# State products with swapped operands in a fused attention and state-space kernel, and another choice of VectorE's share of the exponentials

## The chip, the core and the metric

The kernel runs on one core of a Trainium2 chip. The core has five engines that run side by side, each through its own queue and in order: TensorE (PE, matrix products into PSUM), VectorE (DVE), ScalarE (ACT), GpSimd (POOL) and SyncE (SP, which here issues the DMAs). The metric is the device time of one execution in microseconds; lower is better. Runs of one kernel are summed up by their median.

## The reference

A gate `g` mixes the output of an attention `a` with that of a state-space convolution `b`; both read the same `x` (2048 rows, 512 columns, bfloat16).

```python
g = sigmoid((x * gate_w).sum(-1, keepdims=True))
# a: 32 heads of 16 columns, softmax over 2048 keys
qkv = (x @ wqkv)...; scores = q @ k.T * 16 ** -0.5
a = (softmax(scores) @ v) @ wo
# b: a convolution of every column with a kernel of length 2048
P = exp((dt * A)[:, :, None] * l)          # A complex, 512 x 128 states
K = einsum("dn,dnl,dn->dl", C, P, dt * B).real
b = irfft(rfft(x padded) * rfft(K padded))[:2048] + x * Dskip
out = g * a + (1 - g) * b
```

## The kernel before

**Attention.** The 32 heads run in 32 blocks: a block is 4 heads against 512 queries. A block has 16 key tiles of 128 keys, called quads, since each has 4 tiles of scores (one a head, 128 keys by 512 queries). That makes 2048 tiles. They are worked off in 683 groups of three. In a group TensorE writes three score tiles into one of two PSUM buffers (`SC0`, `SC1`; `qk`), and ScalarE takes the exponentials of all three in one instruction (`ex`, L893) into `ET`. TensorE then multiplies `ET` by the values `VE` and adds up in the PSUM buffer `OA` (`pv`, `pv_mm`). Block 0 to 31 follow one another, 21.3 groups each. At a block's end VectorE transposes and normalises (`norm_a`, `norm_b`, `norm_c`).

**VectorE's sets.** Some quads are not done by ScalarE. VectorE computes the exponentials' bit patterns: one `tensor_scalar` for each of the four tiles from PSUM to a buffer `DZ` (`bits`, L927), and two more passes over all four (`batch`, L938) that give two shifted patterns. The three patterns are multiplied by `VE` and by two scaled copies of it (`VS`, made in `vscaled`) and added. Four groups in a row give one of their three tiles to VectorE, and ScalarE's instruction has two tiles there. Which quads may be taken is set by `VKT` (positions in a block), `WIN` (ranges of group numbers with the number of `DZ`/`DU` buffer pairs in each), `LEFT` (so many quads must be left in the block) and `DVQ`: the planner keeps count of VectorE's idle time in its own cost model, and a set is begun when the unspent idle time reaches a price. The price depends on which flag has been set: first .7, after `S15` (all state products done) 1.2, after `scan0` 2.0, after `scan1` .4 (`decide`, `clear`, `quad`).

**The state-space part** runs beside it, in the gaps. The sequence is cut into 32 chunks of 64 positions; the 512 columns are cut into 16 blocks of 32. First VectorE computes powers of the state factors (`params`, `base`, `table`): a table `PT` a block, written to memory (`ptd`, L1203) and read back transposed as `Qt` (`qload`). `kstage` makes the convolution's kernel within a chunk (`K0` to `K15`). `sstage` makes the state that each chunk adds: products of `Qt` with chunks of `x` (`X2`) into the PSUM buffer `MB`, four times a block ("banks"); VectorE multiplies by the signs `sgn` and writes `Sst` (L1264), a DMA writes that to `sd` in memory (L1270), and when a block is complete `sload` reads it back by a DMA transpose (L1290) into `SG0` or `SG1`, eight blocks each, which hold for every chunk two rows of `SGH` elements. `scan` then runs over the chunks on VectorE, first over `SG0` (`scan0`), then over `SG1` (`scan1`), and replaces each chunk's addition by its state. `ystage` multiplies the states by `Py` (read from `ptd`) and adds the products within a chunk (`Tt`, `XY`), in 32 units; VectorE evicts (L1399). At the end the two halves are mixed (L1525, L1538, L1719).

**Order.** A Python program writes all five queues ahead of time. Each stage is a generator ("thread") with a priority; it yields segments with an engine and an estimated cost, and conditions (`AFTER` a flag, `LOCK` on `MB`). After each group, `Sched.fill` issues the segments that fit before ScalarE's next instruction by estimated times. TensorE gets products of zeros (`zero`) up to a wanted amount of work a group (`FILL`); in groups below 425 whose number modulo 14 is below 4 (`REST`), no segment of priority 2 or 5 goes to TensorE, and the wanted amount is 1792. `place` lays the buffers into SBUF by the first and last group that uses them.

Of the kernel before, what the change touches and what calls it, by code (L numbers as in the profile page):

```python
# [13 lines left out]
P = 128  # L14
# [14 lines left out]
REST = (14, 4, 1792, 425)  # L29
# [7 lines left out]
SGH = 272  # L37
# [3 lines left out]
VKT = (1, 5, 9, 13)  # L41
SHAPE = ((2, 1),) * 4
LEFT = 4
VSW = 152
VSP = len(VKT) * VSW
# [363 lines left out]
def declare(nc, es):  # L409
# [11 lines left out]
    sb("VS", 2 * 4 * VSP)  # L421
    sb("ET", NS * 512)
    for w, (_, _, n) in enumerate(WIN):
        for r in range(n):
            sb(f"DZ{w}{r}", 2048)
            sb(f"DU{w}{r}", 2048)
# [61 lines left out]
    sb("Sst", 4 * 512)  # L488
# [19 lines left out]
    for n, free in (("ptd", NBLK * P * 2 * CB * T), ("sd", D * NCH * 2 * P),  # L508
                    ("kpd", NBLK * P * 8 * P), ("xrd", S * D), ("ytd", D * S), ("qd", D * S), ("od", D * S)):
        B[n] = Buf(n, "dr", free, BF16)  # L510
        B[n].t = nc.dram_tensor("gm_" + n, [free // P, P], BF16)
# [95 lines left out]
def record(nc, p, B, ins):  # L607
    KT, Qm, VE, VS, ET, OT, ON, Rz = (B[n] for n in ("KT", "Qm", "VE", "VS", "ET", "OT", "ON", "Rz"))
    OnT = [B[f"OnT{k}"] for k in range(4)]
    OA, MB = B["OA"], B["MB"]  # L610
    SC = [B["SC0"], B["SC1"]]
# [126 lines left out]
    todo, pend, rem, ends = [], [], [], {}  # L738
    plan = dict(b=-1, at=0, used=0.0, prev=None, wait=None, set=None, k=0)
# [7 lines left out]
    def win(x):  # L747
        return next((w for w, (lo, hi, _) in enumerate(WIN) if lo <= x < hi), None)

    def clear(x):  # L750
        w = win(x)
        if w is None or len(rem) < LEFT + 1 or not any(q % 16 in VKT for q in rem):
            return False
        mine = [i for i, st in enumerate(sets) if st["w"] == w]
        return len(mine) < WIN[w][2] or f"dvp{mine[-WIN[w][2]]}" in sch.flag

    def quad():
        if not rem:
            plan["b"] += 1
            plan["wait"] = None  # L760
            rem.extend(16 * plan["b"] + k for k in sorted(range(16), key=lambda k: (k in VKT, k)))
# [4 lines left out]
        if rem or q < NQ - 16:  # L766
            todo.append((q, plan["prev"], plan["wait"]))
# [15 lines left out]
    def decide(g):  # L783
        while len(tiles) < min(3 * g + 3, NSL):
            x = len(tiles) // 3
            plan["used"] = max(plan["used"], idle() - DVCAP)
            if plan["set"] is None and clear(x) and idle() - plan["used"] >= dvq():
                plan["used"] += dvq()
                c = next(q for q in rem if q % 16 in VKT)
                rem.remove(c)  # L790
# [3 lines left out]
                plan["set"], plan["k"], plan["wait"] = len(sets), 0, f"dvp{len(sets)}"  # L794
# [101 lines left out]
    def pv_mm(s, t, off, R, c, step=None):  # L896
# [6 lines left out]
        else:  # L903
            v, at, rv = VS, (4 * step + pi) * VSP + VKT.index(kt) * VSW, [(VS, (step, pi))]
# [3 lines left out]
    def vscaled():  # L908
        yield ("AFTER", f"g{WIN[0][0] - 12}")
        for pi in range(4):  # L910
            for step, (_, f) in enumerate(STEP):
                yield ("DVE", .3)
                op("DVE", lambda v, pi=pi, step=step, f=f: v.tensor_scalar(VS((4 * step + pi) * VSP, [[VSW, len(VKT)], [1, VSW]]),
                                                                           VE(pi * 4 * VG + VKT[0] * VW, [[VG, len(VKT)], [1, VSW]]), f, None, ALU.mult),
                   [(VE, (pi, x)) for x in range(16)], [(VS, (step, pi))], c=.3)
        sch.mark("VS")
# [16 lines left out]
    def batch(i):  # L933
# [17 lines left out]
        yield ("AFTER", "VS")  # L951
# [293 lines left out]
    Sst, sd = B["Sst"], B["sd"]  # L1245

    def sstage(blk):
        yield ("AFTER", f"ub{blk // 4}")
        q0, qr, bl = (blk % 2) * PTN, blk // 4, blk % 4
        for bank in range(4):  # L1250
            if blk:
                yield ("AFTER", f"sd{blk - 1}.{bank}")
            yield ("LOCK", "MB")
            for pp in range(2):
                yield ("PE", .2)
                for j in range(4):
                    k, par = 4 * bank + 2 * pp + j // 2, j % 2
                    mm(lambda pp=pp, j=j: MB(256 * pp, [[1, 256]], 32 * j, 32),
                       lambda k=k, par=par: X2[qr](16 * bl + k, [[64, 32]], 64 * par, 64),
                       lambda k=k, par=par: Qt(q0 + 128 * k, [[16 * 128, 2], [1, 128]], 64 * par, 64),  # L1260
                       [(Qt, (blk % 2, k // 8), blk), (Qt, (blk % 2, 2 + k // 8), blk), (X2[qr], par)], [(MB, 0, ('S', blk, bank))], pos=(64 * par, 32 * j),
                       c=.19 if j == 0 else 0, a=32, cfg="H")
            yield ("DVE", .65, -1)
            op("DVE", lambda v, bank=bank: v.tensor_tensor(Sst(512 * bank, [[256, 2], [1, 256]]), MB(0, [[256, 2], [1, 256]]),  # L1264
                                                           B["sgn"](0, [[0, 2], [1, 256]]), ALU.mult),
               [(MB, 0, ('S', blk, bank)), (B["sgn"], 0)], [(Sst, bank, (blk, bank))], c=.605)
            sch.unlock("MB")

            def put(bank=bank):
                dma("SP", lambda e, bank=bank: e.dma_start(sd.dram((CB * blk + 8 * bank) * 8192, [[256, P], [4 * 8192, 2], [1, 256]]),  # L1270
                                                           Sst(512 * bank, [[256, 2], [1, 256]])),
                    [(Sst, bank, (blk, bank))], [(sd, (blk, bank))], c=1., lat=3.)
# [484 lines left out]
```

## Time and profile before

| | us |
|---|---|
| median of 3 runs | 861.26 |
| lowest, highest | 856.72, 862.4 |
| the profiled execution, whole | 858.9 |
| its span in the profile | 857.1 |
| ScalarE busy | 832.4 |
| VectorE busy | 764.3 |
| TensorE busy (matmul) | 731.9 |

The profile is that of one execution. A row of a group of instructions gives line, engine, operation, output and inputs with shapes, the count after an x, then busy time and mean duration in ns, then the idle time just before them and what ended it. Instructions of one engine overlap at their ends, so the pace, start to start, is shorter than a duration. Rows of the chain of waits in order of time give start, length, engine, tile and line. Most TensorE work has the line of one helper, L622, and is told apart by its tiles; "wm" is the tile of zeros.

### The profile page before, as it was taken

Reading aid. Unit: us, or ns where it says so; the run is one execution under the profiler, and the core shown is the slowest. Engines: PE = TensorE matmul, PEld = TensorE weight load, DVE = VectorE, ACT = ScalarE, POOL = GpSimd, SP = SyncE. Lnnn points to the kernel's source line nnn. Section 1 sums busy time; section 2 is a strip of 40 time slices with the busy share of each in tenths; the row PEclk is TensorE's granted clock in tenths of the full one; section 3 lists DMA queues with packets and bytes.
Section 4 is the critical chain, followed back from the end, with each engine's and each line's share of the span. In section 5 each row is a group of like instructions: output and inputs, shape, how many; then the busy total and the mean of one; then the engine's idle time right before and its main releaser. Section 6 shows DMA issues by size and latency. Waiting matters only on the chain.

```text
span 857.1 us, 23180 instructions
## 1 busy us (share of the span) xinstructions
PE 731.9 (85%) x10092; PEld 254.9 (30%) x10092; DVE 764.3 (89%) x1290; ACT 832.4 (97%) x693; POOL 11.3 (1%) x15
## 2 busy tenths in 40 slices
PE   7888888888888888888888888789997999999985
PEld 3232332223222222222222222244442323433321
DVE  5899999999989969896989999999999888778794
ACT  7999999999999997999998999999999999999995
POOL 4000000000000000000000000000000000000000
PEclk9999999999999998999997999999999999999998
DMA  9400001961785997999994363856565316444130
GB/s 203 121 2 10 11 16 39 214 193 45 117 207 182 180 201 147 240 147 256 175 145 87 82 111 84 149 138 143 147 150 125 111 38 151 106 93 112 26 99 25
DMA packets 256037, 103.40 MB, mean 121 GB/s; under 512 B 214337, under 2 KB 242881, under 8 KB 253889
## 3 DMA queue, kind: packets, MB, share of 16 engines
q1 hardware_dynamic: 254208, 101.02, 53.5%
q8 instruction: 79, 1.29, 0.7%
q10 hardware_dynamic: 1728, 0.92, 0.4%
q14 instruction: 22, 0.17, 0.1%
HBM read 35.17 MB, written 39.20 MB: 87 GB/s over the span
## 4 chain that ended last, share of the span: by engine, by line
ACT 84%; DVE 8%; PE 4%; DMA 3%; issue 1%; SPq 0%; ACTq 0%; DVEq 0%
ACT ET L893 84%; DVE DZ L927 2%; PE SC L622 2%; PE OA L622 1%; DMA gm_ptd<-PT 1%; DVE AR L1525 1%; DVE Sst L1264 1%; DMA gm_sd<-Sst 1%; DMA Wq<-in_A_wqkv_dram 1%; DMA SG<-gm_sd 1%; DVE DZ L938 1%; DVE s L1320 0%; PE MB L622 0%; DVE s L1315 0%; DVE G L1323 0%
## 5 line engine op out<-in xcount | busy, mean ns | idle before, releaser
L893 ACT ACTIVATE ET<-SC 128x1536 bf16<-128x1536 f32 (+1 forms) x683 | 825.2, 1572 | 11.2 <-PE SC L622 8.7
L622 PE MATMUL SC<-Qm,KT 32*128 32x512 bf16 x2048 | 273.4, 387 | 99.1 <-ACT ET L893 82.4
L622 PE MATMUL OA<-wm 128*32 128x256 bf16 (+3 forms) x2556 | 276.3, 343 | 1.2 <-DVE wm L675 1.2
L622 PE MATMUL OA<-ET,VE 128*32 128x512 bf16 x1828 | 183.8, 393 | 0.6 <-ACT ET L893 0.6
L927 DVE TENSOR_SCALAR DZ<-SC 128x512 uint16<-128x512 f32 x220 | 145.4, 685 | 24.4 <-PE SC L622 23.4
L622 PEld LDWEIGHTS SC<-Qm,KT 32*128 32x128 bf16 x2048 | 70.1, 91 | 326.5 <-ACT ET L893 279.0
L622 PEld LDWEIGHTS OA<-wm 128*32 128x32 bf16 (+2 forms) x2556 | 81.4, 95 | 41.3 <-issue 22.9
L622 PEld LDWEIGHTS OA<-ET,VE 128*32 128x32 bf16 x1828 | 46.9, 93 | 105.1 <-issue 98.9
L1264 DVE TENSOR_TENSOR Sst<-MB,sgn 128x512 bf16<-128x512 f32 x64 | 43.8, 684 | 5.5 <-DMA gm_sd<-Sst 2.8
L938 DVE TENSOR_SCALAR DZ<-DZ 128x2048 uint16<-128x2048 uint16 x55 | 37.8, 688 | 7.5 <-PE OA L622 7.2
L1323 DVE TENSOR_TENSOR G<-s,s 128x512 f32<-128x512 f32 x60 | 41.2, 687 | 1.1
L1315 DVE TENSOR_TENSOR s<-G,MU 128x512 f32<-128x512 f32 x60 | 41.1, 685 | 0.0
L1320 DVE TENSOR_TENSOR s<-s,SG 128x512 f32<-128x512 f32 x60 | 41.1, 685 | 0.0
L1317 DVE TENSOR_TENSOR s<-G,MU 128x512 f32<-128x512 f32 x60 | 41.0, 683 | 0.0
L938 DVE TENSOR_SCALAR DU<-DZ 128x2048 uint16<-128x2048 uint16 x55 | 37.7, 687 | 0.2
L980 DVE TENSOR_TENSOR ft<-FP,L 128x1024 f32<-128x1024 f32 (+1 forms) x32 | 34.5, 1086 | 0.1
L622 PE MATMUL MB<-Qt,X 64*32 64x256 bf16 x512 | 31.5, 307 | 3.0 <-DVE Sst L1264 2.6
L980 DVE TENSOR_TENSOR PT<-tt,tt 128x1024 bf16<-128x1024 bf16 x48 | 33.0, 687 | 0.3
L962 DVE STREAM_TRANSPOSE OT<-OA 128x512 f32<-128x512 f32 x32 | 22.7, 710 | 8.5 <-PE OA L622 8.0
L622 PEld LDWEIGHTS MB<-Py,SG 128*32 128x32 bf16 x1024 | 27.5, 149 | 7.5 <-issue 2.9
L622 PE MATMUL MB<-Py,SG 128*32 128x64 bf16 x1024 | 27.7, 219 | 0.0
L1326 DVE CAST SG<-G 128x512 bf16<-128x512 f32 x60 | 25.5, 425 | 1.5
(160 smaller groups left out, 606.5 us busy)
## 6 DMA issues: line engine op xcount, KB each, us to landing
gm_ptd<-PT SPq DMA_DIRECT2D x16, 1024.0 KB, 6.1
Py<-gm_ptd SPq DMA_DIRECT2D x32, 512.0 KB, 4.2
gm_sd<-Sst SPq DMA_DIRECT2D x64, 128.0 KB, 3.6
gm_kpd<-Kst SPq DMA_DIRECT2D x16, 256.0 KB, 3.8
Tt<-gm_kpd SPq DMA_DIRECT2D x128, 32.0 KB, 3.3
gm_xrd<-in_A_x_dram SPq DMA_DIRECT2D x1, 2048.0 KB, 12.2
X<-gm_xrd SPq DMA_DIRECT2D x8, 256.0 KB, 4.1
Wo<-in_A_wo_dram SPq DMA_DIRECT2D x4, 512.0 KB, 4.1
```

What stands on the lines that cost most here:

```text
L622: op("PE", lambda t: t.matmul(out(), lhsT(), rhs(), start=start, stop=stop, skip_group_check=True, **kw), R, W, c=c, lat=.15, a=a, cfg=cfg)
L893: op("ACT", lambda a: a.activation(ET(512 * e, [[1, 512 * n]]), sc(0, [[1, 512 * n]]), AF.Exp, scale=DH ** -0.5), [(sc, i, g) for i in ran ...
L927: op("DVE", lambda v: v.tensor_scalar(z.u16(512 * k, [[1, 512 * n]]), sc(512 * na, [[1, 512 * n]]), XS, XB, ALU.mult, ALU.add), [(sc, na + ...
L938: op("DVE", lambda v: v.tensor_scalar(t.u16(0, [[1, 2048]]), z.u16(0, [[1, 2048]]), float(STEP[k][0]), None, ALU.add), R, W, c=.07 + 2048 ...
L962: op("DVE", lambda v: v.transpose(OT(512 * w, [[1, 512]]), OA(0, [[1, 512]])), [(OA, 0, b)], [(OT, w, b)], c=.64)
L980: op(eng, lambda v: v.tensor_tensor(o(), a(), b_(), f), R, W, c=c)
L1264: op("DVE", lambda v, bank=bank: v.tensor_tensor(Sst(512 * bank, [[256, 2], [1, 256]]), MB(0, [[256, 2], [1, 256]]), B["sgn"](0, [[0, 2], ...
L1315: op(e, lambda v: v.tensor_tensor(s2(0, W), G(0, W), MU(d0, [[0, 2], [1, 256]]), ALU.mult), key("G", "MU"), [(s2, 0)], c=F5)
L1317: op(e, lambda v: v.tensor_tensor(s3(0, W), G(256, [[-256, 2], [1, 256]]), MU(D + d0, [[D, 2], [1, 256]]), ALU.mult), key("G", "MU") + [(M ...
L1320: op(e, lambda v, so=so: v.tensor_tensor(s2(0, W), s2(0, W), sg(so, [[SGH, 2], [1, 256]]), ALU.add), [(s2, 0)] + ks, [(s2, 0)], c=F5)
L1323: op(e, lambda v: v.tensor_tensor(G(0, [[1, 512]]), s2(0, [[1, 512]]), s3(0, [[1, 512]]), ALU.add), [(s2, 0), (s3, 0)], [(G, 0)], c=F5)
L1326: op(e, lambda v, so=so: v.tensor_copy(sg(so, [[SGH, 2], [1, 256]]), G(0, W)), key("G"), ks if c < NCH - 2 else [(sg, k, (h, 'G')) for k i ...
```

## The change

- `sstage` swaps the operands: `Qt` (128 columns) becomes the weights and `X2` (32 columns, 64 elements apart) the moving operand, so that the output has the states on the partitions. A block has 64 products of 32 columns instead of 32 of 256; a bank's 16 all use one half of the rows. VectorE's eviction writes from `MB` straight into `SG`, 32 chunks that lie 2 x `SGH` elements apart. `Sst`, `sd`, its writes and `sload` go. `SGH` falls from 272 to 256. The first half's products wait for group 195, the second's for group 260.
- A second list of key tiles, `(3, 7, 11)`, with a second scaled buffer `VS1`, holds from group 640; `clear` also takes a tile of the next block when fewer quads than wanted are left. From group 430 to 640 there are two `DZ`/`DU` pairs instead of three. `LEFT` is 3, the prices are 0.7, 2.0, 0.8 and 0.2, and the two passes of a set have a lower priority (`BUP`).
- `REST` never holds. The loads for `ystage` wait for `S12` instead of `K15`.

```diff
-REST = (14, 4, 1792, 425)
+REST = (14, 0, 1792, 425)
...
-SGH = 272
+SGH = 256
+SGAT = (195, 260)
+SMM = .035
...
-VKT = (1, 5, 9, 13)
+VKT = ((1, 5, 9, 13), (3, 7, 11))
 SHAPE = ((2, 1),) * 4
-LEFT = 4
+LEFT = 3
...
+VSAT = (178, 600)
-WIN = ((190, 430, 2), (430, 676, 3))
-DVQ = (("scan1", .4), ("scan0", 2.0), ("S15", 1.2), (None, .7))
+WIN = ((190, 430, 2, 1), (430, 640, 2, 1), (640, 676, 3, 2))
+DVQ = (("scan1", 0.2), ("scan0", 0.8), ("S15", 2.0), (None, 0.7))
...
-BUP = 0
+BUP = 1
...
+    def keys(x):
+        w = win(x)
+        return () if w is None else sum(VKT[:WIN[w][3]], ())
...
-        if w is None or len(rem) < LEFT + 1 or not any(q % 16 in VKT for q in rem):
+        if w is None or keytile(x) is None:
...
+    def block(b):
+        ks = keys(len(tiles) // 3 + 4)
+        return [16 * b + k for k in sorted(range(16), key=lambda k: (k in ks, k))] if b < 32 else []
+
+    def keytile(x):
+        of = rem if len(rem) > LEFT else ahead
+        return next(((of, q) for q in of if q % 16 in keys(x)), None)
...
     def sstage(blk):
-        yield ("AFTER", f"ub{blk // 4}")
-        q0, qr, bl = (blk % 2) * PTN, blk // 4, blk % 4
-        for bank in range(4):
-            if blk:
-                yield ("AFTER", f"sd{blk - 1}.{bank}")
-            yield ("LOCK", "MB")
-            for pp in range(2):
-                yield ("PE", .2)
-                for j in range(4):
-                    k, par = 4 * bank + 2 * pp + j // 2, j % 2
-                    mm(lambda pp=pp, j=j: MB(256 * pp, [[1, 256]], 32 * j, 32),
-                       lambda k=k, par=par: X2[qr](16 * bl + k, [[64, 32]], 64 * par, 64),
-                       lambda k=k, par=par: Qt(q0 + 128 * k, [[16 * 128, 2], [1, 128]], 64 * par, 64),
...
+        yield ("AFTER", f"ub{qr}")
+        yield ("AFTER", f"g{SGAT[h]}")
...
+        for bank in range(4):
+            yield ("LOCK", "MB")
+            par, k0 = bank % 2, bank // 2 * 8
+            for part in range(2):
+                yield ("PE", 8 * SMM)
+                for j in range(8):
+                    k = k0 + j
+                    mm(lambda part=part, j=j: MB(256 * part + 32 * j, [[1, 32]]),
+                       lambda k=k, par=par, part=part: Qt(q0 + 2048 * part + 128 * k, [[1, 128]], 64 * par, 64),
+                       lambda k=k, par=par: X2[qr](16 * bl + k, [[64, 32]], 64 * par, 64),
...
+            yield ("DVE", .65, -1)
+            op("DVE", lambda v, bank=bank: v.tensor_tensor(sg(2 * SGH + CB * k8 + 2 * (bank // 2 * 8) + bank % 2, [[SGH, 2], [2, 8], [2 * SGH, 32]]),
+                                                           MB(0, [[256, 2], [32, 8], [1, 32]]), B["sgn"](0, [[128, 2], [0, 256]]), ALU.mult),
...
-    def sload(blk):
-        qr, bl = divmod(blk, 4)
-        for i in range(4):
-            yield ("AFTER", f"sd{blk}.{i}")
-        yield ("AFTER", "S15" if qr > 1 else "K9")
...
-        dma("SP", lambda e: e.dma_start_transpose(sg(2 * SGH + CB * k, [[SGH, 64], [1, CB]]),
-                                                  sd.dram(CB * blk * 8192, [[8192, CB], [1, 8192]])),
...
     def yloads():
-        yield ("AFTER", "K15")
+        yield ("AFTER", "S12")
```

More of the change, by code (lines that the diff above doesn't have):

```diff
@@ L737, in record @@
     tiles, sets, vec, home, held = [], [], {}, {}, {}
[L738 to L739 removed]
+    todo, pend, rem, ahead, ends, dvps = [], [], [], [], {}, {}
+    plan = dict(b=-1, at=0, used=0.0, prev=None, set=None, k=0)
     def idle():
@@ L759, in quad @@
             plan["b"] += 1
-            plan["wait"] = None
-            rem.extend(16 * plan["b"] + k for k in sorted(range(16), key=lambda k: (k in VKT, k)))
+            rem.extend(ahead or block(plan["b"]))
+            ahead[:] = block(plan["b"] + 1)
         q = rem.pop(0)
@@ L1293, in sload @@
+        sch.mark(f"S{blk}")
         sch.mark(f"sg{blk}")
```

83 lines of the change are left out of this document (36 added, 47 removed).

## The prediction

> **What bounds the kernel now.** I read the page's chain of waits first, then its groups by form.
>
> ```profile
> span 857.1 us, 23180 instructions
> ...
> ACT 84%; DVE 8%; PE 4%; DMA 3%; issue 1%; SPq 0%; ACTq 0%; DVEq 0%
> ...
> L893 ACT ACTIVATE ET<-SC 128x1536 bf16<-128x1536 f32 x462 | 628.4, 1771 | 3.5 <-PE OA L622 2.1 <-PE SC L622 1.2
> ...
> L893 ACT ACTIVATE ET<-SC 128x1024 bf16<-128x1024 f32 x221 | 214.4, 1156 | 7.6 <-PE SC L622 7.5
> ...
> L927 DVE TENSOR_SCALAR DZ<-SC 128x512 uint16<-128x512 f32 x220 | 145.4, 685 | 24.4 <-PE SC L622 23.4
> ...
> 14.84 200.11 ACT ET L893 x149
> ```
>
> ScalarE's exponentials are the chain: 683 groups of three key tiles, of which 220 gave one tile to VectorE (four of these make a set: 55 sets). The last line, from the chain in order of time, is an unbroken run of three-tile groups: 200.11/149 = 1.343 us each. ScalarE can only get shorter in two ways: fewer tiles, or fewer waits. Next, windows by stage.
>
> ```profile
> 301.00:344.00 43.00, 35.92 (x474) 10.94 (x474) 34.29 (x58) 38.66 (x33) 0.00 (x0) 0.92 0.86 180
> ...
> 387.00:430.00 43.00, 36.99 (x499) 11.74 (x491) 36.50 (x64) 41.99 (x38) 0.00 (x0) 1.00 0.93 207
> ...
> 430.00:473.00 43.00, 37.35 (x435) 10.95 (x432) 38.54 (x67) 39.53 (x32) 0.00 (x0) 0.88 0.70 112
> ...
> 559.00:602.00 43.00, 38.61 (x777) 18.02 (x781) 42.22 (x78) 43.00 (x34) 0.00 (x0) 1.00 0.63 149
> ...
> 668.00:797.00 129.00, 119.88 (x1907) 46.93 (x1911) 105.09 (x177) 129.00 (x127) 0.00 (x0) 1.00 0.40 97
> ...
> 797.00:857.00 60.00, 44.85 (x571) 13.60 (x559) 44.29 (x66) 48.86 (x46) 0.00 (x0) 0.95 0.18 52
> ```
>
> Columns: TensorE matmul, weight load, VectorE, ScalarE, GpSimd, granted clock, DMA share, GB/s. ScalarE is full except in three stretches, all in the stage of the state products: 4.34 + 1.01 + 3.47 = 8.8 us lost, twice with the clock down. VectorE has 129 - 105.09 = 23.9 us free at 668 to 797, after the scan. That is where sets could still go.
>
> ```profile
> 306.34 0.39 PE SC L622 x3
> ...
> 310.87 0.46 PE MB L622 x8
> ...
> 313.44 7.62 DMA gm_ptd<-PT
> ...
> 393.91 5.31 DMA SG<-gm_sd
> ...
> 438.31 5.59 DMA gm_sd<-Sst
> ...
> DVE PT L1186 <- DMA gm_ptd<-PT: 5.8, 3, 2.9
> ...
> DVE Sst L1264 <- DMA gm_sd<-Sst: 2.8, 1, 2.8
> ...
> DVE G L1312 <- DMA SG<-gm_sd: 1.9, 2, 1.2
> ```
>
> The chain names a transfer ahead of each of the three losses: VectorE, which keeps its order, stood behind a DMA, and the evictions that ScalarE's PSUM bank needs stood behind VectorE.
>
> **The change, part by part.** The round trip through memory goes.
>
> ```profile
> L1270 SPq DMA_DIRECT2D gm_sd<-Sst x64: 372/488/1859, 173.3 to 529.4; - x64
> ...
> L1290 SPq DMA_TRANSPOSE SG<-gm_sd x16: 1430/2571/6942, 281.3 to 548.3; - x16
> ...
> gm_ptd<-PT SPq DMA_DIRECT2D x16, 1024.0 KB, 6.1
> ```
>
> Removed: 64 writes and the 16 transposes that read them, 64 x 0.488 + 16 x 2.571 = 72 us of SP's queue between 173 and 548 us. Two of the three transfers in the chain no longer exist. The third, the write of PT (median 6.1 us to landing, 7.62 in the chain), shares the engines and SP's queue with them at a DMA share of 0.86 to 0.93. So these losses should go. What is late next in each place is TensorE, which the chain shows from 306.3 to 311.3 us, just ahead of the first loss; so I count 7 of the 8.8 us.
>
> TensorE: 512 products of 256 columns become 1024 of 32 columns with 128 columns of weights. Nothing of that shape runs before; nearest are the gate's products, with full weights and one moving column.
>
> ```profile
> 204.91 0.35 PE L622 MATMUL MB<-gwT,xT 128*128 128x1 bf16 x8
> ...
> 205.20 0.40 PE L622 MATMUL OA<-wm 128*32 128x512 bf16 x4
> ...
> 284.12 0.45 PE L622 MATMUL MB<-Qt,X 64*32 64x256 bf16 x8
> ...
> L622 PEld LDWEIGHTS MB<-gwT,xT 128*128 128x128 bf16 x64 | 2.1, 96 | 1.8 <-issue 1.8
> ...
> PE SC L622 <- ACT ET L893: 36.0, 109, 0.7
> ```
>
> Eight gate products take 205.20 - 204.91 = 0.29 us to the next instruction, 36 ns each, though each weight load lasts 96 ns: loads overlap. At that pace the new products take 1024 x 0.036 = 37 us; the old ones 64 x 0.45 = 29 us. The extra 8 us is covered by the 36.0 us that TensorE waits for ScalarE between 215 and 530 us (last line). Were no load hidden, the price would be 1024 x 0.096 = 98 us; were they faster than one gate product, at most those 8 us of covered time come back, worth nothing. I take 36 ns.
>
> The Trainium skill (TensorE: Matmul & The Clock Gate, Part 3, on what overlaps) says that a weight load overlaps a running matmul only when the row group differs. All sixteen products of a bank use the same 64 rows, so by it every load would be exposed. The gate's rows, one row group throughout, do not agree: 0.29 us for eight is a third of eight loads.
>
> VectorE: still 64 evictions, now with stores 1,024 bytes apart.
>
> ```profile
> L1264 DVE TENSOR_TENSOR Sst<-MB,sgn 128x512 bf16<-128x512 f32 x64 | 43.8, 684 | 5.5 <-DMA gm_sd<-Sst 2.8 <-PE MB L622 2.2 <-PE SC L622 0.4
> ...
> L1139 DVE COPY FP<-VV 128x256 f32<-128x256 f32 x4 | 1.6, 400 | 0.0
> ...
> L1399 DVE TENSOR_TENSOR Yst<-MB,gt 128x256 bf16<-128x256 f32 x32 | 13.4, 418 | 9.1 <-PE MB L622 9.1
> ...
> L622 PEld LDWEIGHTS MB<-Py,SG 128*32 128x32 bf16 x1024 | 27.5, 149 | 7.5 <-issue 2.9
> ```
>
> L1139 stores 256 single elements 32 bytes apart in 400 ns, no longer than the dense 256 of L1399 (418). So 0.684 us stays, and the cost is 0. The other end is the only strided access here that is slower, the weight load from SG: 149 ns against the 96 of the gate's dense load, 1.55 times; at that ratio 64 x 0.38 = 24 us. A gain is excluded: the same 512 elements come out of PSUM.
>
> The Trainium skill (SBUF — State Buffer, Door 1: The DMA port swizzle) says that each access that crosses to a new 16-byte line pays a penalty; that speaks against this layout. L1139 crosses one with every store and shows none; the strided weight load does show one.
>
> Sets: what one is worth, and how many more.
>
> ```profile
> L927 DVE TENSOR_SCALAR DZ<-SC x96: 652/687/695, 669.9 to 792.3; 128x512 uint16<-128x512 f32 x96
> ...
> L927 DVE TENSOR_SCALAR DZ<-SC x12: 652/684/692, 571.5 to 659.9; 128x512 uint16<-128x512 f32 x12
> ...
> L927 DVE TENSOR_SCALAR DZ<-SC x28: 651/685/692, 800.9 to 837.7; 128x512 uint16<-128x512 f32 x28
> ...
> 743.79 0.69 DVE L938 TENSOR_SCALAR DU<-DZ 128x2048 uint16<-128x2048 uint16 x1
> 744.39 1.29 DVE L927 TENSOR_SCALAR DZ<-SC 128x512 uint16<-128x512 f32 x2
> ...
> L913 DVE TENSOR_SCALAR VS<-VE 128x608 bf16<-128x608 bf16 x8 | 2.4, 316 | 0.0
> ```
>
> At 668 to 797 there are 127 groups, 96 with a VectorE tile: (129 - 31 x 1.343)/96 = 0.910 us for a two-tile group. A tile moved saves 1.343 - 0.910 = 0.433, a set 1.73 us. It costs VectorE six passes at 0.60 us start to start: 3.6 us.
>
> The second key-tile list holds only from group 640; the last 46 groups lie after 797 us, so it covers about the last 40 us. A set spreads over four groups, so 36 groups take 9 sets where 7 (28 tiles) ran: +2. Between groups 430 and 640 the list has four tiles a block as before, 24 sets in six blocks, already at its cap; tiles of the next block shift these sets, not their number, and two buffers instead of three can only hold them back. The rest must come from the second half's scan, where the price of a set in idle time falls from 2.0 to 0.8: 3 sets ran in 555 to 668 us; at 2.0 these used 6 us of planned idleness, at 0.8 that buys 7; VectorE is near full there, so I take +3. Between the last product and the first scan the price rises from 1.2 to 2.0: -1. Sum +4, 4 x 1.73 = 6.9 us. The ends are -2 (the dearer price and the fewer buffers bind) and +9: 23.9 us of free VectorE over 3.6 gives 6.6, and the two at the end. The second list's eight scalings cost 8 x 0.3 = 2.4 us, inside the 23.9.
>
> Edits at no cost: the Y loads now wait for the thirteenth block's products instead of the last K; their first user waits for the first half's scan, and SP is 72 us lighter. The dense rests before group 425 go; at 559 to 602, where small products run without rests, the clock is 1.00; if it fell, a loss like the 4.34 or 3.47 us above returns each time. Gating the first products to group 195 moves the first of them later; the table still paces the rest.
>
> Sum on the profiled execution: 857.1 - 7.0 - 6.9 = 843.2 us span, and 1.8 around it (858.9 - 857.1): 845.0. The median of the runs shown, 861.26, lies 2.4 higher, so I say **847**.
>
> **Rivals.** One of them rests on the end of the run:
>
> ```profile
> L1399 DVE TENSOR_TENSOR Yst<-MB,gt x2: 424/424/425, 798.8 to 806.3; 128x256 bf16<-128x256 f32 x2
> ...
> 828.83 18.22 ACT ET L893 x16
> ```
>
> A: the waits go, but sets do not rise (the four-tile cap stays to group 640): 847 + 6.9 = 854. For it: that cap; against: the cheaper price in the scan. B: VectorE's free time is really used, nine more sets: 847 - 5 x 1.73 = 838. C, slower: TensorE becomes the bound in the product stage, because loads of 128 columns in one row group, or moving columns 128 bytes apart, are not hidden. Its place is TensorE's queue between two scores; at 96 ns a product it holds 98 - 29 = 69 us more, 36 of them covered, so ScalarE waits 33 us: 847 + 33 = 880. It makes the kernel slower by over 1% from (870 - 847 + 36 + 29)/1024 = 86 ns a product on; the gate's 36 ns speaks against. D: the scan ends later, for added sets and late gating, and the Y units (last eviction at 806 us, the exponentials end at 847) become the tail: some 25 us of slide are free, each further one costs itself; at 40 us 847 + 15 = 862. E: slow strided stores: with VectorE near full, 24 us less some 10 us of the waits that leave: 861.
>
> **How the numbers follow.** Chances: forecast 0.50 (840 to 852), A 0.17, B 0.10, C 0.12, D 0.06, E 0.05. The likeliest value is 847. The range 835 to 868 takes in A, B, D and E and leaves out C and the edges. This kernel's runs differ by 0.7%, so 1% is about what can be told: 852.6 and 869.9 are the bounds. Faster: 0.48 of the forecast, B, and 0.05 of A: 0.63. Slower: 0.11 of C, 0.03 of D, 0.02 of E: 0.16. Within 1%: 0.21.
>
> **What would show it.** No ScalarE window below 43 between 301 and 473; no clock dip; L1264's successor at 0.68 us; eight state products in 0.29 us; L927 counted about 236. Wrong if products take 60 ns or more, if new waits for MB or SG head the chain, or if L927 stays at 220.

## The result, and the profile after

The changed kernel takes 989.5 us (median of 4 runs, 986.42 to 991.02) against 861.23 before: 1.150 times as long, 95% interval 1.147 to 1.153. The prediction said 847 us, with 835 to 868 as its range. The profiled execution took 989.78 us. Of the runs further on, two of e3's five, one of e5's ten and one of e16's six were slower than the others of their kernel, and medians and ratios leave them out, though the profiles of e3 and e5 are of such a run. The page of the changed kernel:

```profile
span 988.0 us, 23445 instructions
...
ACT 54%; DVE 26%; PE 17%; issue 1%; DMA 1%; ACTq 0%; DVEq 0%
...
L944 DVE TENSOR_SCALAR DZ<-SC 128x512 uint16<-128x512 f32 x228 | 159.0, 716 | 20.0 <-PE SC L625 19.1
L1286 DVE TENSOR_TENSOR SG<-MB,sgn 128x512 bf16<-128x512 f32 x64 | 156.5, 2445 | 11.1 <-PE MB L625 10.7
...
L625 PEld LDWEIGHTS MB<-Py,SG 128*32 128x32 bf16 x1024 | 42.0, 220 | 7.5 <-issue 5.5
```

The chain has moved from ScalarE (84% before) to VectorE and TensorE. The new eviction (L1286) takes 2,445 ns where the old one took 684: 64 x 1.76 = 113 us more of VectorE. The weight loads of the `ystage` products also changed, from 149 ns to 220. VectorE's tiles rose from 220 to 228, two sets more. The same windows as before:

```profile
301.00:344.00 43.00, 38.39 (x403) 14.14 (x399) 41.49 (x45) 30.28 (x24) 0.00 (x0) 0.64 0.50 107
387.00:430.00 43.00, 39.27 (x413) 13.67 (x409) 40.65 (x50) 33.28 (x27) 0.00 (x0) 0.70 0.57 110
...
559.00:602.00 43.00, 42.27 (x403) 14.92 (x400) 41.26 (x47) 29.93 (x23) 0.00 (x0) 0.50 0.66 109
```

ScalarE (fourth number) is busy 30 to 33 us of 43 where it was busy 39 to 43, VectorE (third) is nearly full, and the granted clock is 0.50 to 0.70 where it was 0.92 to 1.00. In the views of waits, first before and then after, ScalarE's wait for scores grew from 8.7 us, 9 times, to 105.0 us, 135 times:

```profile
ACT ET L893 <- PE SC L622: 8.7, 9, 3.8
```

```profile
ACT ET L908 <- PE SC L625: 105.0, 135, 2.7
```

Where the time went is best told by ScalarE's own pace. For each of the 682 steps from the end of one exponential to the end of the next, I take off the pace of the prediction (1.343 us with three tiles, 0.910 with two); what is left is lost time. Worked out so from the traces, in us:

```
kernel  first end  at full pace  lost in groups 0-200  200-440  440-682  after the last  span
before     12.4       820.2             1.2              10.8      3.2        9.1        857.1
after      14.3       816.8             4.9             118.3     24.3        9.4        988.0
```

So there are two losses: 107.5 us in the stage of the state products (groups 200 to 440), and 21 us in the stage of the Y units (440 to 682), which the prediction did not have at all.

### The profile page after: what moved, and what is told of

Its sections match the earlier page's. It is cut to its first block, busy times and chain, and to the rows that moved or that the text cites. A ratio compares the mean times of both kernels' runs of the same rounds, so it can differ in the third digit from the quotient of the medians.

```text
span 988.0 us, 23445 instructions
## 1 busy us (share of the span) xinstructions
PE 851.9 (86%) x10276; PEld 314.3 (32%) x10276; DVE 904.9 (92%) x1310; ACT 867.1 (88%) x693; POOL 11.3 (1%) x15
## 4 chain that ended last, share of the span: by engine, by line
ACT 54%; DVE 26%; PE 17%; issue 1%; DMA 1%; ACTq 0%; DVEq 0%
ACT ET L908 54%; DVE SG L1286 12%; PE OA L625 7%; PE SC L625 6%; PE MB L625 5%; DVE DZ L944 3%; DVE G L1321 2%; DVE s L1315 1%; DVE s L1313 1%; DVE s L1318 1%; DVE tt L997 1%; DVE SG L1324 1%; DVE OT L979 1%; DVE DZ L955 1%; DMA Wq<-in_A_wqkv_dram 1%
## 5 line engine op out<-in xcount | busy, mean ns | idle before, releaser
L908 ACT ACTIVATE ET<-SC 128x1536 bf16<-128x1536 f32 (+1 forms) x683 | 860.0, 1534 | 106.7 <-PE SC L625 105.0
L625 PE MATMUL SC<-Qm,KT 32*128 32x512 bf16 x2048 | 308.0, 430 | 95.0 <-ACT ET L908 77.0
L625 PE MATMUL OA<-wm 128*32 128x512 bf16 (+3 forms) x2208 | 292.6, 395 | 1.2 <-DVE wm L678 1.2
L625 PE MATMUL OA<-ET,VE 128*32 128x512 bf16 x1820 | 201.2, 436 | 1.1 <-DVE OT L979 0.8
L944 DVE TENSOR_SCALAR DZ<-SC 128x512 uint16<-128x512 f32 x228 | 159.0, 716 | 20.0 <-PE SC L625 19.1
L1286 DVE TENSOR_TENSOR SG<-MB,sgn 128x512 bf16<-128x512 f32 x64 | 156.5, 2445 | 11.1 <-PE MB L625 10.7
L625 PE MATMUL MB<-X,Qt 64*128 64x32 bf16 x1024 | 73.7, 230 | 22.1 <-DVE SG L1286 21.6
L625 PEld LDWEIGHTS MB<-X,Qt 64*128 64x128 bf16 x1024 | 58.9, 115 | 60.0 <-issue 44.0
L625 PEld LDWEIGHTS MB<-Py,SG 128*32 128x32 bf16 x1024 | 42.0, 220 | 7.5 <-issue 5.5
L625 PE MATMUL MB<-Py,SG 128*32 128x64 bf16 x1024 | 41.0, 262 | 0.3 <-issue 0.3
```

The source lines that it names most:

```text
L625: op("PE", lambda t: t.matmul(out(), lhsT(), rhs(), start=start, stop=stop, skip_group_check=True, **kw), R, W, c=c, lat=.15, a=a, cfg=cfg)
L908: op("ACT", lambda a: a.activation(ET(512 * e, [[1, 512 * n]]), sc(0, [[1, 512 * n]]), AF.Exp, scale=DH ** -0.5), [(sc, i, g) for i in ran ...
L944: op("DVE", lambda v: v.tensor_scalar(z.u16(512 * k, [[1, 512 * n]]), sc(512 * na, [[1, 512 * n]]), XS, XB, ALU.mult, ALU.add), [(sc, na + ...
L1286: op("DVE", lambda v, bank=bank: v.tensor_tensor(sg(2 * SGH + CB * k8 + 2 * (bank // 2 * 8) + bank % 2, [[SGH, 2], [2, 8], [2 * SGH, 32]]) ...
```

## The experiments

All ratios are to the kernel before on the same chip, with 95% intervals.

### The eviction's stores: e1, e2, e3, e4

**e1** lets the same eviction write the same number of elements to adjacent places.

```diff
-sg(2 * SGH + CB * k8 + 2 * (bank // 2 * 8) + bank % 2, [[SGH, 2], [2, 8], [2 * SGH, 32]])
+sg(2 * SGH + 512 * (4 * k8 + bank), [[256, 2], [1, 256]])
```

> The changed kernel, but each eviction of state products writes the same 512 values densely into the scan's buffer, so they land in the wrong places (the states, and with them the state-space half of the output, are wrong). Theory 1, the stores 1,024 bytes apart are the cost: the eviction falls from 2.44 to 0.68 us, the clock stays up through the stage of the products, and the time comes down to 845 to 865 us. Rival 2, the missing rests and the state products at 69 ns instead of the planned 35 pull the clock down: the eviction falls to 0.68 us, but the clock still goes to half many times between 300 and 680 us and the time stays over 900. Rival 3, the sign operand read with step zero is the cost: the eviction stays at 2.4 us and the time at 985 to 990.

Measured: 880.95 us, ratio 1.019 (1.016 to 1.023). From its page, and one of its windows:

```profile
L1286 DVE TENSOR_TENSOR SG<-MB,sgn 128x512 bf16<-128x512 f32 x64 | 44.0, 687 | 8.6 <-PE MB L625 7.4
...
L625 PEld LDWEIGHTS MB<-Py,SG 128*32 128x32 bf16 x1024 | 42.0, 220 | 6.7 <-issue 4.8
```

```profile
301.00:344.00 43.00, 42.02 (x566) 18.54 (x563) 40.50 (x69) 42.44 (x37) 0.00 (x0) 1.00 0.74 146
```

Dense stores alone take away 108.6 of the 128 us. ScalarE is full again, and the clock is 1.00 from 198 to 850 us although there are no rests: the low clock of the changed kernel followed from the late VectorE. How much of the 107.5 us goes through that low clock, and how much through VectorE's queue alone, these runs do not separate. What is left is the slow weight load, untouched at 220 ns; for it the time stayed above the 845 to 865 us that were expected.

**e2** changes the row pitch alone.

```diff
-SGH = 256
+SGH = 264
```

> The changed kernel with rows of the scan's buffer of 264 elements instead of 256, so the stores of an eviction are 1,056 bytes apart; all else the same. Theory 1a, a store of two bytes that goes to another place far away each time is slow whatever the step: eviction 2.4 us, time 985 to 990. Theory 1b, only a step of a power of two is slow (the stores meet in the same part of the memory): eviction 0.68 us, time 845 to 865; the loads of weights from the same buffer would also come back from 217 to about 149 ns.

Measured: 961.92 us, ratio 1.114 (1.109 to 1.118).

```profile
L1286 DVE TENSOR_TENSOR SG<-MB,sgn 128x512 bf16<-128x512 f32 x64 | 150.4, 2351 | 11.5 <-PE MB L625 11.0
...
L625 PEld LDWEIGHTS MB<-Py,SG 128*32 128x32 bf16 x1024 | 27.4, 148 | 9.5 <-issue 5.1
```

The stores stay slow, 1,056 bytes apart as 1,024; the `ystage` loads are back at 148 ns, and 28 us are gone. These are two separate things, so neither theory had all of it.

**e3** writes the same places in another order: the innermost loop goes over eight elements 4 bytes apart, then to the next chunk.

```diff
-sg(2 * SGH + CB * k8 + 2 * (bank // 2 * 8) + bank % 2, [[SGH, 2], [2, 8], [2 * SGH, 32]])
...
-MB(0, [[256, 2], [32, 8], [1, 32]])
+sg(2 * SGH + CB * k8 + 2 * (bank // 2 * 8) + bank % 2, [[SGH, 2], [2 * SGH, 32], [2, 8]])
...
+MB(0, [[256, 2], [1, 32], [32, 8]])
```

> The changed kernel with the two inner loops of the eviction exchanged: eight stores 4 bytes apart, then the next chunk 1,024 bytes on; the reads from PSUM are now 128 bytes apart. The result is the reference's. Theory 1 (far steps between stores are the cost, one far step in eight remains): eviction 0.7 to 0.95 us, time 845 to 875. If reads from PSUM 128 bytes apart cost as much: eviction 2 us or more, time near 990. Rival 3 (the sign operand): 2.4 us.

Measured: 878.83 us, ratio 1.019 (1.013 to 1.024).

```profile
L1286 DVE TENSOR_TENSOR SG<-MB,sgn 128x512 bf16<-128x512 f32 x64 | 46.8, 731 | 14.7 <-PE MB L625 13.7
```

The same bytes in another order cost almost nothing, so it is the step from one store to the next that costs. The time stays a little above the 845 to 875 us expected, for the same loads as in e1.

**e4** reads the sign operand densely in place of one value repeated.

```diff
-B["sgn"](0, [[128, 2], [0, 256]])
+B["sgn"](0, [[0, 2], [1, 256]])
```

> The changed kernel with the sign operand of the eviction read densely (256 elements with step one, twice) instead of one element repeated; the signs are then wrong, so the state-space half of the output is. Theory 1: no change, 2.4 us an eviction and 985 to 990 us. Rival 3: 0.68 us and 845 to 865 us.

Measured: 989.7 us (one run), the eviction 2,450 ns. The sign operand plays no part.

### The price by itself: m1, m2

**m1** is a kernel of its own: eight evictions for each step between stores, 512 bf16 values from PSUM on each partition, and some rows of matmuls.

> No part of the kernel: a row of single instructions, eight of each, that measure the disputed prices by themselves (the output is zeros). VectorE multiplies 512 values from PSUM by a bfloat16 operand and stores 2-byte values with steps of 2, 4, 8, 16, 32, 64, 128, 256, 512, 1,024, 1,056 and 1,088 bytes between neighbours, and with runs of 2, 4, 8 and 16 values 1,024 bytes apart; then copies, a read 1,024 bytes apart, ScalarE's store, and TensorE's weight loads at steps of 2, 128, 1,024, 1,056 and 1,088 bytes and state products with dense and spread moving columns. Theory A (every store to a new 16-byte line is slow): 0.68 us up to 8 bytes, a jump at 16 bytes, then flat at 2.4. Theory B (only far steps): 0.68 up to some step of 64 to 512 bytes, 2.4 from there on; L1139 of the kernel before, free at 32 bytes, speaks for B. Runs of 8: 0.75 to 0.95 in both. Products: if the spread moving columns are the reason for 69 ns, dense ones take 36; if the load of 128 columns in one row group is, both take 69 and the gate's shape 36.

Groups of its profile (busy time, mean ns of one). The steps of L512 to L530 are 2, 4, 8, 16 and 1,024 bytes; L536 stores pairs of adjacent values, 1,024 bytes from pair to pair; L546 reads at a step of 1,024 and stores densely; L550 and L552 are ScalarE's stores at 1,024 bytes and dense.

```profile
L550 ACT ACTIVATE Z<-MB 128x512 bf16<-128x512 f32 x8 | 19.6, 2446 | 249.6 <-DVE D L548 249.4
...
L530 DVE TENSOR_TENSOR Z<-MB,sgn 128x512 bf16<-128x512 f32 x8 | 19.5, 2432 | 0.3
L518 DVE TENSOR_TENSOR Z<-MB,sgn 128x512 bf16<-128x512 f32 x8 | 19.4, 2420 | 0.3
...
L516 DVE TENSOR_TENSOR Z<-MB,sgn 128x512 bf16<-128x512 f32 x8 | 10.3, 1292 | 0.3
...
L514 DVE TENSOR_TENSOR Z<-MB,sgn 128x512 bf16<-128x512 f32 x8 | 5.8, 728 | 0.3
L512 DVE TENSOR_TENSOR Z<-MB,sgn 128x512 bf16<-128x512 f32 x8 | 5.5, 691 | 2.0 <-issue 1.7
L536 DVE TENSOR_TENSOR Z<-MB,sgn 128x512 bf16<-128x512 f32 x8 | 5.5, 691 | 0.3
...
L552 ACT ACTIVATE Z<-MB 128x512 bf16<-128x512 f32 x8 | 4.8, 597 | 0.3
L546 DVE COPY D<-Z 128x512 bf16<-128x512 bf16 x8 | 4.7, 589 | 0.3
...
L580 PE MATMUL OA<-Q 64*128 64x32 bf16 x64 | 3.9, 231 | 0.0
...
L576 PE MATMUL OA<-wm,Q 64*128 64x32 bf16 x64 | 1.8, 173 | 0.0
```

A lone 2-byte store costs next to nothing extra up to 4 bytes from the last one, (1,292 - 691)/512 = 1.2 ns at 8 bytes, and from 16 bytes on the full price, (2,432 - 691)/512 = 3.4 ns each, much the same at every distance. Two adjacent values that begin at a multiple of 4 bytes are as cheap as a dense run. It is a matter of writing: the read at the same step takes 589 ns in all. And it is not of VectorE alone: ScalarE pays (2,446 - 597)/512 = 3.6 ns. The last two rows are the state products with moving columns 128 bytes apart (3.9 us for 64) and adjacent (1.8): the spread moving operand makes them slow, not the weight loads in one row group, which are the same in both.

**m2** asks whether the width of the value matters, and what the row pitch does to weight loads in four column tiles at once.

> No part of the kernel: single instructions again (the output is zeros). VectorE stores 4-byte values with steps of 4, 8, 16, 32, 64 and 1,024 bytes, and pairs of 2-byte values 1,024 bytes apart that do not begin at a multiple of 4 bytes. Theory W (a lone store narrower than 4 bytes is what is slow): all 4-byte steps at 0.69 us, as L1139 of the kernel before suggests, and the shifted pairs slow. Theory L (any store to a new 16-byte line): 4-byte stores slow from 16 bytes on. TensorE: four products in the four column tiles at a time, weights at steps of 1,024, 1,040, 1,056 and 1,088 bytes. Theory P (a pitch of 1,024 bytes makes the four loads meet): 1,024 slower than 1,056 and 1,088 by about a third; rival, the slow loads of the Y stage need the traffic of the whole kernel: all the same.

L514, L516, L518 and L522 are float32 stores 8, 16, 32 and 1,024 bytes apart; L524 stores pairs of 2-byte values 1,024 bytes apart that begin 2 bytes past a multiple of 4; L553 and L558 are weight loads at 1,024 and 1,056 bytes.

```profile
L524 DVE TENSOR_TENSOR Z<-MB,sgn 128x512 bf16<-128x512 f32 x8 | 12.6, 1580 | 0.2
...
L518 DVE TENSOR_TENSOR F<-MB,sgn 128x512 f32<-128x512 f32 x8 | 8.6, 1077 | 0.3
L516 DVE TENSOR_TENSOR F<-MB,sgn 128x512 f32<-128x512 f32 x8 | 8.4, 1056 | 0.3
L522 DVE TENSOR_TENSOR F<-MB,sgn 128x512 f32<-128x512 f32 x8 | 8.1, 1016 | 0.3
...
L514 DVE TENSOR_TENSOR F<-MB,sgn 128x512 f32<-128x512 f32 x8 | 5.5, 691 | 0.3
...
L553 PEld LDWEIGHTS OA<-Q,Z 128*32 128x32 bf16 x64 | 1.9, 239 | 0.4 <-issue 0.4
...
L558 PEld LDWEIGHTS OA<-Q,Z 128*32 128x32 bf16 x64 | 1.1, 162 | 0.4 <-issue 0.4
```

A 4-byte store far from the last one pays (1,016 - 691)/512 = 0.6 ns, a fifth of what a 2-byte store pays, so both theories were half right. Pairs off a multiple of 4 bytes take 1,580 ns where m1's pairs took 691, so where a pair begins matters too. And four column tiles whose weights lie 1,024 bytes apart load slower than at 1,056 bytes; in m1, with one column tile, 1,024 and 1,056 bytes took the same (149 and 158 ns).

### Both repairs, and each half alone: e5, e6, e10

**e5** is e3 and e2 together.

> Both repairs at once: the eviction's inner loop over eight stores 4 bytes apart, and rows of the scan's buffer of 264 elements (1,056 bytes from chunk to chunk). The result is the reference's. Theory: the far stores cost the stage of the products and, separately, the pitch of 1,024 bytes costs the Y stage (weight loads 217 ns instead of 140, some 24 us in groups 440 to 680). Then the eviction takes 0.73 us, the weight loads 140 ns, and the time comes to 850 to 862 us, near the kernel before. Rival: the Y stage was slow for the late scan, not for the pitch; then the time stays at 875 to 885.

Measured: 858.34 us, ratio 0.996 (0.993 to 0.998), the eviction 736 ns and the `ystage` loads 148. The two repairs together bring the changed kernel back to the time before.

**e6** has the kernel before's products, `SGH` and rests with the changed sets (lists, windows, prices, `LEFT`, `BUP`).

> The kernel before with the new choice of sets alone (second list, next block's tiles, prices, buffers, priority); products, round trip through memory, row pitch and rests as before. Theory: 57 or 58 sets instead of 55 at 1.7 us each, minus what denser sets cost in waits: 856 to 864 us against 861 to 863, no difference that can be told. Rival, that the sets themselves cost (two buffers instead of three, lower priority): over 870.

Measured: 870.68 us, ratio 1.010 (1.007 to 1.013), with 232 tiles on VectorE. The last exponential ends at 841.6 us, 6.4 us earlier than before, but the span is 8.2 us longer: 23.6 us follow it, where 9.1 did. The chain in order of time shows what:

```profile
842.03 5.27 DMA Wo<-in_A_wo_dram
...
849.66 1.47 PE MB L626 x3
...
856.52 0.63 DVE OT L980
```

The last load of `Wo`, the mixing of the halves and the last block's normalisation queue up behind a VectorE that got to the Y units later (its last eviction of them starts at 834.2 us, before at 806.3). So the 856 to 864 us expected were missed, by the tail and not by waits for the sets.

**e10** is the other half: e5's products, without rests, with the old sets.

```diff
-VKT = ((1, 5, 9, 13), (3, 7, 11))
+VKT = ((1, 5, 9, 13),)
...
-WIN = ((190, 430, 2, 1), (430, 640, 2, 1), (640, 676, 3, 2))
-DVQ = (("scan1", 0.2), ("scan0", 0.8), ("S15", 2.0), (None, 0.7))
+WIN = ((190, 430, 2, 1), (430, 676, 3, 1))
+DVQ = (("scan1", .4), ("scan0", 2.0), ("S15", 1.2), (None, .7))
```

> The changed products and direct stores with both repairs, no rests, but the sets chosen as before. Theory: the DMA waits of the product stage (8.8 us) go, the products at 69 ns and the clock give some of it back: 852 to 864 us. Rival, that products at 69 ns and the missing rests pull the clock down for long: over 875 with the clock at half between 300 and 550 us.

Measured: 868.24 us, ratio 1.007 (1.004 to 1.010), with 216 tiles, above the 852 to 864 us expected. Groups 200 to 440 still lose 11.5 us, in many small waits for TensorE: the DMA waits are gone and the stage is no faster.

### What the product stage still loses: e12, e16, e17, e18

**e12** adds to e5 what m1 asks for: GpSimd copies each quarter of `x` so that the 32 moving columns lie side by side.

```diff
+op("POOL", lambda g, qr=qr: g.tensor_copy(B[f"XD{qr}"](0, [[32, 64], [1, 32]]), X2[qr](0, [[1, 64], [64, 32]])),
...
```

> Both repairs of the stores and the pitch as before, and the moving columns of the state products laid densely: GpSimd, idle until then, copies each quarter of x's chunks into that order once. The result is the reference's. By the single instructions (64 products in 3.9 us with columns 128 bytes apart, in 1.8 us with dense ones) eight products should take 0.28 us instead of 0.55, as planned. Theory: the waits that were left in the product stage (15 us of lateness in groups 280 to 360) come from products that are later than the plan; then 843 to 853 us, below the kernel before. Rival, they come from the evictions at 0.73 us on a full VectorE or from the missing rests: 855 to 862, no better than with spread columns.

Measured: 860.76 us, ratio 0.999 (0.997 to 1.002). Eight products now take 310.72 - 310.43 = 0.29 us, as was forecast, but groups 200 to 440 lose 10.6 us, now in three clumps, and the 843 to 853 us expected did not come. The timeline at the first:

```profile
310.27 4.80 DVE L998 TENSOR_TENSOR tt<-B,D32.2_152 128x1024 bf16<-128x1024 bf16 x2
...
310.43 0.36 PE L626 MATMUL MB<-XD,Qt 64*128 64x32 bf16 x8
310.68 3.84 POOL L1433 COPY XD<-X 128x2048 bf16<-128x2048 bf16 x1 [38.00 <-DMA X<-gm_xrd]
310.72 0.10 PEld L626 LDWEIGHTS OA<-wm 128*32 128x32 bf16 x4
```

Two VectorE operations of 0.68 us take 4.80: the second stands still until the copy ends. The other two clumps begin likewise behind the copies at 382.15 and 444.26 us.

**e16** cuts the copy into sixteen pieces, one a block; a piece waits for the last product that read its slot, so it starts as the block's last eviction does.

```diff
+op("POOL", lambda v, qr=qr, bl=bl, blk=blk: v.tensor_copy(B["XD"](512 * (blk % 2), [[32, 16], [1, 32]]), X2[qr](16 * bl, [[1, 16], [64, 32]])),
...
-        yield ("AFTER", "S12")
+        yield ("AFTER", "S13")
```

> e12 with its relaying of x cut into sixteen pieces: GpSimd copies the 16 columns of one block (512 elements, four times shorter than before) into a buffer of two slots, two blocks ahead of their use; the Y loads wait for S13 in place of S12, for room. In e12 ScalarE lost 3.4, 2.8 and 3.3 us between groups 200 and 440, each time right behind one of the GpSimd copies of 3.7 to 4.1 us that start at 310.7, 382.2 and 444.3, while a VectorE operation of 0.69 us took about 4.2. Theory H: a GpSimd copy holds VectorE for its whole length, and these three holds are all that is left of the loss, so the round trip's 7 us would be saved if the relaying cost VectorE nothing. Pieces of about 1 us are short enough for the two buffers of scores to hide: ScalarE's loss between groups 200 and 440 falls from 12 to about 4 us, last exponential near 840, ratio about 0.99. Rival F: VectorE has no spare time in that stage, and its total of some 15 us counts, not its pieces: the loss stays at 10 to 12 us and the ratio at 1.00. Either way VectorE's operations beside a piece should take about 1.6 us in place of 0.69.

Measured: 852.93 us, ratio 0.988 (0.985 to 0.990). **e18** is the same kernel once more, for a trace.

> e16 once more, for a trace: the profiled execution of e16 took 1227.7 us while its five timed runs took 850.0 to 856.1. By theory H ScalarE's loss between groups 200 and 440 is about 4 us, where e12 lost 12, and each VectorE operation beside a piece takes about 1.6 us; the ratio is again near 0.99. By rival F the loss is 10 us or more, and e16's gain lies elsewhere (in the tail, or in the groups before 200).

Measured: 851.7 us, ratio 0.987 (0.984 to 0.990): the fastest kernel here, 1.3% below the kernel before. From its page, and the timeline at a piece:

```profile
span 850.2 us, 23478 instructions
...
L1287 DVE TENSOR_TENSOR SG<-MB,sgn 128x512 bf16<-128x512 f32 x64 | 46.9, 732 | 1.2 <-PE MB L626 1.0
L626 PE MATMUL MB<-XD,Qt 64*128 64x32 bf16 x1024 | 40.7, 174 | 0.0
```

```profile
438.73 1.29 POOL L1441 COPY XD<-X 128x512 bf16<-128x512 bf16 x1 [9.01 <-PE MB L626]
438.97 0.75 DVE L1287 TENSOR_TENSOR SG<-MB,sgn 128x512 bf16<-128x512 f32 x1
439.61 0.96 DVE L1319 TENSOR_TENSOR s<-s,SG 128x512 f32<-128x512 f32 x1
```

Groups 200 to 440 lose 5.1 us, half of before's 10.8 and of e12's 10.6, near the 4 us of theory H. The Y loads also wait for one block more than in e12, and no run tells the two apart. That operations beside a piece would take 1.6 us was wrong: the eviction, which reads PSUM, runs at its usual 0.75, and only the next operation, with both inputs in SBUF, is held 0.3 us. The Trainium skill (SBUF — State Buffer, section SBUF: two separate sides) has it that a VectorE operation with two SBUF inputs and a GpSimd operation that reads SBUF exclude each other for a whole instruction; these rows agree. A VectorE copy with one SBUF input was held as well: beside the first copy of e12 one (`PT<-B`, at 134.14 us) took 3.33 us.

**e17** lets VectorE itself copy the pieces; for room the second half's products wait for group 308.

> As e16, but VectorE itself copies the sixteen pieces (a strided read of 512 bf16 took 0.589 us by itself in m1), so 16 x 0.59 = 9.4 us of VectorE in place of four holds of 3.7 to 4.1 us; the second half's products wait for group 308 in place of 260, for room. Theory H: 9.4 us in short pieces are hidden, loss between groups 200 and 440 about 4 us, ratio 0.985 to 0.99. Rival F: the loss falls only in proportion to VectorE's time, from 12 to about 8 us, ratio 0.995. If the later gate makes the Y units late, the last exponential shows the gain and the tail behind it (9.1 us in e12) takes it back.

Measured: 858.85 us, ratio 0.994 (0.992 to 0.996). Groups 200 to 440 lose 8.0 us, 4.7 of them in groups 312 to 317, just where the later gate opens, and it has only 216 tiles. It neither bears out nor refutes what was expected of VectorE's copies, since the gate moved both.

### More sets on top of e12: e14, e15

**e14** lets the second list begin at group 600 (`WIN`, `VSAT`); **e15** gives e12 short rests, `REST = (14, 2, 1792, 425)`. Both have 236 tiles in place of 228.

> As the run with dense moving columns, and the second list of key tiles allowed from group 600 instead of 640: 59 sets instead of 57. Theory: 2 sets x 1.7 us = 3 us less than that run: 840 to 850 us. Rival (VectorE too full near the end, the Y units or the exponentials wait): the same or slower.

> As the run with dense moving columns, with dense rests again in two of every 14 groups before group 425 (59 sets by the plan). Theory: rests do not matter where the evictions are quick, apart from the one clock dip at 200 us that the changed kernel and all its repairs show (about 3 us): within 5 us of that run. Rival, the clock needs them: 8 us or more faster, and no dip between 200 and 500 us.

Measured: 862.75 us, ratio 1.001 (0.998 to 1.003), and 870.15 us, ratio 1.010 (1.006 to 1.014). The last exponential ends at 842.4 and 843.8 us where e12's ended at 848.2; what follows it takes 14.5 and 25.5 us in place of 9.1. As in e6, what more sets save is given back in the tail, and in e15 more than that; both were expected to do better.

## Why the Y stage got slower

The loads of 220 ns are not themselves the loss: TensorE has room there. Window 570 to 720, e1 (1,024 bytes):

```profile
570.00:720.00 150.00, 128.06 (x2076) 55.85 (x2075) 144.39 (x235) 150.00 (x115) 0.00 (x0) 1.00 0.48 115
```

and e12 (1,056 bytes), with the same sets:

```profile
570.00:720.00 150.00, 132.06 (x2256) 52.92 (x2248) 143.55 (x253) 150.00 (x127) 0.00 (x0) 1.00 0.52 122
```

ScalarE is never idle in either, and yet it does 115 exponentials in one and 127 in the other (80 and 81 of them with three tiles). It runs slower. So does VectorE; the timeline of e1, and all runs of one scan step in e1 and then in e18 (least, median and most ns):

```profile
601.57 0.68 DVE L1318 TENSOR_TENSOR s<-s,SG 128x512 f32<-128x512 f32 x1
...
602.29 1.28 DVE L1321 TENSOR_TENSOR G<-s,s 128x512 f32<-128x512 f32 x1
...
602.61 0.79 PEld L625 LDWEIGHTS MB<-Py,SG 128*32 128x32 bf16 x24
```

```profile
L1321 DVE TENSOR_TENSOR G<-s,s x60: 649/692/1299, 428.1 to 705.8; 128x512 f32<-128x512 f32 x60
```

```profile
L1322 DVE TENSOR_TENSOR G<-s,s x60: 646/691/695, 422.4 to 687.7; 128x512 f32<-128x512 f32 x60
```

The step that takes 1.28 us is the one beside 24 of these weight loads. Worked out over the whole trace: the median time from end to end of three-tile exponentials without a gap, by the number of `Py,SG` loads beside each:

```
loads beside it     0      1-8    9-16   17 or more
after, 1,024 bytes  1343   1489   1742   1884 ns
e18,   1,056 bytes  1343   1343   1344   1344 ns
```

And by pitch, the time lost in groups 440 to 682: 24.3 (after), 24.4 (e1), 24.3 (e3) and 23.9 (e4) at 1,024 bytes; 3.6 (e2), 3.7 (e5), 3.4 (e10), 3.4 (e12) and 3.5 us (e18) at 1,056; 3.2 before, at 1,088. Of the 24.3 us, the 75 exponentials with such loads beside them make up 21.1, and in e18 the 75 lose 0.3. So loading weights at a step of 1,024 bytes slows what ScalarE and VectorE do at the time, and that costs 21 us; the pitch without such loads beside it (column 0) costs nothing. What in the memory makes them meet is not shown by these runs. The Trainium skill (SBUF — State Buffer, section Who interferes with whom) says that only the port pair of VectorE and GpSimd makes engines wait for each other; these rows disagree.

## Why the prediction was wrong

**The step that failed** is the eviction's price: "So 0.684 us stays, and the cost is 0." It took L1139's 400 ns as the nearest row for strided stores. That row stores 4-byte values; the eviction stores 2-byte values. By m2 and m1 these differ fivefold in what a far store adds: for L1139's 256, 32 bytes apart, an estimate from m2's 1,077 ns is 256 x 0.75 ns = 0.19 us, which the comparison with a PSUM eviction (418 ns) did not bring out; the eviction's 512 pay 1.74. The other end, 1.55 times, came from a weight load, a read; m1's strided read took 589 ns for 512, less than a dense eviction. So the range of 0 to 24 us left out the 113 that came, and rival E, the right mechanism, had too small a price (861) and a chance of 0.05. The Trainium skill (SBUF — State Buffer, Door 1), which asks for at least two accesses in each 16-byte line, was set aside on that one row; for 2-byte stores m1's step of 16 bytes (2,420 ns) and its pairs at full speed agree with it, but its step of 8 bytes, two stores in a line, takes 1,292 ns and does not.

**A step that was missing:** `SGH` from 272 to 256 appears among the changes, and no term of the sum prices it. It cost 21 us, more than any gain in the sum.

**The round trip's waits**, 7 of 8.8 us: in the changed kernel the DMAs are gone from the chain, but nothing is saved, since the evictions are late. In e18 the loss falls by 5.7 us, near the term; but e18 also has both repairs, dense columns and later Y loads, so the nearness may be luck. With spread columns e1 saves 2.0 us (8.8 lost) and e10 nothing (11.5).

**Products at 36 ns, covered by waiting time:** the pace was wrong, the cover right for the most part. Timeline of the changed kernel:

```profile
394.87 0.62 PE L625 MATMUL MB<-X,Qt 64*128 64x32 bf16 x8
395.42 0.10 PEld L625 LDWEIGHTS OA<-wm 128*32 128x32 bf16 x4
...
396.96 2.46 DVE L1286 TENSOR_TENSOR SG<-MB,sgn 128x512 bf16<-128x512 f32 x1
```

Eight take 395.42 - 394.87 = 0.55 us, 69 ns each: the gate's products, from which 36 was taken, move one column, and m1 puts the difference down to the spread of the 32. That is 1024 x 0.033 = 34 us more of TensorE, and e1, which has it, is all but full on ScalarE at 301 to 344 us (42.44 of 43) and loses 8.8 us in groups 200 to 440, less than before; e18, without it, loses 5.1. Rival C (33 us, from 86 ns on) did not come about. What the prediction feared if no load were hidden, 98 us, did not appear either: in m1 64 full loads and products in one row group take 1.8 us, 28 ns each.

**Sets:** +2, not +4, worth 820.2 - 816.8 = 3.4 us as 8 tiles x 0.433 says. The price of a set was right, the count twice what came.

**The rests, at no cost:** nearly. Without them groups 0 to 200 lose 4.9 us in the changed kernel against 1.2, in one short dip, but 2.7 in e18; the deep fall of the clock from 300 us on goes with the slow stores (e1: 1.00).

**The tail** (rival D) stayed at 9.4 us in the changed kernel; in e6, e14 and e15 it was real, 14.5 to 25.5 us, and it is what limits more sets.

With stores, loads and products near the prices of the sum, e18 has a span of 850.2 us where the sum said 843.2. The 7.0 between are, by the terms, the waits (5.7 saved in place of 7.0), the sets (3.4 in place of 6.9), 1.5 lost before group 200, and about 1 in the start, the Y stage and the tail.

## What to carry to other kernels

A neighbouring row is a price only if its element width, its direction (read or write) and its step are those of the new instruction; where one differs, the price is open and the range must hold what a few ns for each element would cost. Every constant in a diff that sets an address, a row pitch above all, needs its own term, for all engines that read the buffer later and for those that work beside them. And where the order of a strided write is free, let the innermost loop take the smallest step: here that alone was worth some 110 us.

## What was not expected of the hardware

- Lone 2-byte stores 16 bytes or more apart take some 3.4 ns more each on VectorE (2,432 against 691 ns for 512) and 3.6 on ScalarE (2,446 against 597); pairs pay nothing if they begin at a multiple of 4 bytes (691) and much if they do not (1,580); 4-byte stores pay 0.6 ns at 1,024 bytes (1,016).
- Weight loads at a step of 1,024 bytes in four column tiles take 220 ns in place of 148 and slow the other engines meanwhile: ScalarE's exponential from 1,343 to 1,884 ns beside 17 or more, VectorE's scan step from 692 to 1,299 at most.
- A moving operand with columns 128 bytes apart doubles a product of 32 columns (3.9 against 1.8 us for 64).
- A GpSimd copy of 3.84 us held a VectorE operation with two SBUF inputs for its whole length; one of 1.29 us did not hold a VectorE operation that reads PSUM and writes SBUF.
